# VectorE writes the result buffers once more ahead of the branch, and takes the minimum of the sums' test alone

## The chip, the cores and the metric

The kernel runs on one core of one Trainium2 chip. The core has five engines with a queue of instructions each: TensorE (PE in the profile: matrix products), VectorE (DVE), ScalarE (ACT), GpSimd (POOL) and SyncE (SP, which here issues nearly all transfers). They run on their own and wait for each other by semaphores. Transfers between the core's memory SBUF and the chip's memory are carried by 16 DMA engines; a transfer raises its semaphore by 16, one update from each. The metric is the device time of one execution in microseconds (us), as the median of several.

## The reference

One transformer block on 2048 rows of 448 numbers in bf16: a sliding-window attention and a gated feed-forward layer side by side, on the same normalised input.

```python
x = A_x
xn = _layernorm(x, axis=-1)
return x + _A_ref(xn, A_wqkv, A_wo) + _B_ref(xn, B_w_gate, B_w_up, B_w_down)
```

`_A_ref` has 16 heads of 28 columns; a row sees itself and the 255 rows before it, and the softmax of the scaled scores weighs v. `_B_ref` is `(gelu(x @ w_gate) * (x @ w_up)) @ w_down` with 1792 hidden columns.

## The kernel before

The rows are worked through in four blocks (`qb`) of 512. For each block the kernel computes the scores and their exponentials, multiplies with v, and computes the feed-forward layer's hidden columns (`hT`). The down projection of a block, which also takes in the attention's output projection, runs one block later beside the next one's attention, and for the last block at the very end. The order of the work on each engine is written out by hand (the pools are opened under `manual_schedule`), with generators that give out the work of TensorE in pieces of some 370 ns.

The softmax skips the usual subtraction of the row's maximum. That is right only while the sums of the exponentials stay in a range, so the kernel keeps all of them (`l_all`, 128 x 256) and tests them at the end. If any lies outside, it recomputes everything by `general_path`, a long second program under `tc.If`, which overwrites the output. With these inputs it doesn't run. The instructions of that program lie between the branch and the end of the kernel, so every engine has to jump over them.

The end of the kernel before goes like this:

- VectorE makes the test's 0 or 1 for every sum, and the minimum of each of the 128 partitions (`okc`, lines 802 to 805), and turns it into bf16 (`okb`, 806).
- `gen_down` gives the last block's down projection (lines 358 to 382): for each of four tiles of 128 rows 4 matmuls with `wo` (line 370) and 14 with `wd` (375) into one PSUM bank `po`, then VectorE's addition of x into the result buffer `res` (380), then SyncE's store of it (381). There are two `res` buffers, used in turn. The last tile is done in two halves of 224 columns, so the pass has five additions and stores.
- After a third of that work (`share`, then line 810) TensorE sums the 128 minima by a matmul of 1 x 1, `nok`; VectorE turns it into an integer `flag` (812).
- After another third, every engine loads the flag into a register (814, TENSOR_LOAD in the trace). ScalarE and GpSimd, which have no more work, load it and branch at once.
- The rest of the pass runs (`drain`), and each engine takes its branch (line 820). Behind the branch, on the side that skips the general path, every engine raises its own semaphore by as much as the general path would have (EVENT_SEMAPHORE of line 820), and SyncE does so for the eight semaphores of the stores, for each when the transfers so far have landed. Then comes the end of the program (line 927): SyncE waits in eight instructions for all semaphores, two in each, the sixth of which asks for VectorE's; all engines meet twice in a barrier; GpSimd clears the semaphores.

A hint to load the code behind the branch ahead of time stands in line 743, for VectorE and for TensorE.

Of the kernel before, what the change touches and what calls it, by code (L numbers as in the profile page):

```python
# [9 lines left out]
ALU = mybir.AluOpType  # L10
AX = mybir.AxisListType
bf16 = mybir.dt.bfloat16
f32 = mybir.dt.float32
i32 = mybir.dt.int32

S, D, H, Dh, F = 2048, 448, 16, 28, 1792
P = 128
NT = S // P
NF = F // P
QB, NB = 512, 4  # L20
# [34 lines left out]
def share(feeds, first, second):  # L55

    want = [first, second]
    while True:
        can = [i for i, f in enumerate(feeds) if f.gens and want[i] > 190 and not f.held]
        if not can:  # L60
            return
        i = max(can, key=lambda i: (not feeds[i].closed, want[i]))
        for f in feeds:
            if f is not feeds[i]:
                f.closed = False
        want[i] -= feeds[i].run()


def drain(feeds):

    while any(f.gens for f in feeds):
        min((f for f in feeds if f.gens), key=lambda f: (f.held, f.closed)).run()
# [3 lines left out]
def kernel(  # L76
# [11 lines left out]
    nc = tc.nc  # L88
    const = ctx.enter_context(tc.tile_pool(name="const", bufs=1))
# [3 lines left out]
    work = fast.enter_context(tc.tile_pool(name="work", bufs=3))  # L93
# [3 lines left out]
    phase = [None]  # L97
# [253 lines left out]
    DOWN = 4 * 3400  # L351
# [6 lines left out]
    def gen_down(qb, tags):  # L358

        hT, oN = hTs[qb], oNs[qb]  # L360
        for tt in range(4):
            t = 4 * qb + tt
            cs = slice(tt * P, (tt + 1) * P)
            for n, (lo, up) in enumerate(((0, D),) if t < NT - 1 else ((0, D // 2), (D // 2, D))):
                w = up - lo
                tag = tags[tt + n]
                down_tag[0] = tag
                po = psum.tile([P, QB], f32, name="po", tag=tag, bufs=2 if tag == "m" else 1)
                for g in range(4):
                    nc.tensor.matmul(po[:, 0:w], lhsT=oN[:, g, cs], rhs=wo[:, g, lo:up], start=(g == 0), stop=False,  # L370
                                     skip_group_check=True)
                    if g % 2:
                        yield 380 * w // D
                for f in range(NF):
                    nc.tensor.matmul(po[:, 0:w], lhsT=hT[:, f, cs], rhs=wd[:, f, lo:up], start=False, stop=(f == NF - 1),  # L375
                                     skip_group_check=True)
                    if f % 2 and f < NF - 1:
                        yield 375 * w // D
                res = work.tile([P, D], bf16, name="res", bufs=2)
                nc.vector.tensor_tensor(out=res[:, 0:w], in0=po[:, 0:w], in1=x_sb[:, t, lo:up], op=ALU.add)  # L380
                nc.sync.dma_start(out=outv[:, t, lo:up], in_=res[:, 0:w])
                yield 375 * w // D
# [412 lines left out]

    g1 = work.tile([P, 512], f32, name="g1", tag="wc", bufs=1)
    g2 = work.tile([P, 512], f32, name="g2", tag="wb", bufs=1)
    okc = const.tile([P, 1], f32, name="okc")
    okb = const.tile([P, 1], bf16, name="okb")
    one = const.tile([P, 1], bf16, name="one")  # L800
    lf = l_all[:, :, :].rearrange("p a b -> p (a b)")
    nc.vector.memset(one[:, :], 1.0)
    nc.vector.tensor_scalar(out=g1[:, 0:256], in0=lf, scalar1=L_LO, scalar2=None, op0=ALU.is_ge)
    nc.vector.scalar_tensor_tensor(out=g2[:, 0:256], in0=lf, scalar=L_HI, in1=g1[:, 0:256], op0=ALU.is_le, op1=ALU.mult)
    nc.vector.tensor_reduce(out=okc[:, :], in_=g2[:, 0:256], axis=AX.X, op=ALU.min)
    nc.vector.tensor_copy(out=okb[:, :], in_=okc[:, :])
    feed = Feed((gen_down(NB - 1, "dmomd" if last_tag[0] == "o" else "omdmo"), DOWN))
    share([feed], DOWN / 3, 0)
    nok = phase[0].pool.tile([P, 2 * QB], f32, name="nok", tag="s")
    nc.tensor.matmul(nok[0:1, 0:1], lhsT=okb[:, :], rhs=one[:, :], start=True, stop=True)  # L810
    flag = const.tile([1, 1], i32, name="flag")
    nc.vector.tensor_copy(out=flag[:, :], in_=nok[0:1, 0:1])
    share([feed], DOWN / 3, 0)
    n_ok = nc.values_load(flag[0:1, 0:1], min_val=0, max_val=P)
    drain([feed])
    phase[0].close()
    fast.close()


    with tc.If(n_ok < P, preferred_fallthrough_block=True, label="general"):  # L820
        general_path(tc, locals_=dict(x_sb=x_sb, xnT=xnT, qT=qT, kT=kT, v_sb=v_sb, wg=wg, wu=wu, wgu3=wgu3, wd=wd, wo=wo,
                                      ident=ident, outv=outv))

# [108 lines left out]
```

## Time and profile before

| What | us |
|---|---|
| median of 3 runs (lowest, highest) | 223.24 (223.16, 223.36) |
| the profiled execution, its own time | 223.5 |
| its span, first to last instruction | 221.7 |
| TensorE busy in the span | 214.3 |
| VectorE busy | 156.2 |
| VectorE's last addition (392 ns) starts | 217.37 |
| the last store is issued | 217.79 |

The profile is of one execution. Its page has the busy time of each engine, the chain of work that ended last, and the costliest groups of instructions; the trace behind it has every instruction, every DMA packet and every update of a semaphore. Times in it count from the first instruction of the span. Register loads, branches and semaphore instructions don't count as busy; they stand in the trace by their line, with an engine's name that ends in q. The packets of queue 1 are the kernel's own transfers, those of kind "instruction" (queues 8 and 14) are the engines' code. The granted clock of TensorE is 1.000 over the span.

### The profile page before, as it was taken

Reading aid. Unit: us, or ns where it says so; the run is one execution under the profiler, and the core shown is the slowest. Engines: PE = TensorE matmul, PEld = TensorE weight load, DVE = VectorE, ACT = ScalarE, POOL = GpSimd, SP = SyncE. Lnnn points to the kernel's source line nnn. Section 1 sums busy time; section 2 is a strip of 40 time slices with the busy share of each in tenths; the row PEclk is TensorE's granted clock in tenths of the full one; section 3 lists DMA queues with packets and bytes.
Section 4 is the critical chain, followed back from the end, with each engine's and each line's share of the span. In section 5 each row is a group of like instructions: output and inputs, shape, how many; then the busy total and the mean of one; then the engine's idle time right before and its main releaser. Section 6 shows DMA issues by size and latency. Waiting matters only on the chain.

```text
span 221.7 us, 5352 instructions
## 1 busy us (share of the span) xinstructions
PE 214.3 (97%) x2240; PEld 94.9 (43%) x2240; DVE 156.2 (70%) x370; ACT 132.9 (60%) x129; POOL 45.0 (20%) x65
## 2 busy tenths in 40 slices
PE   6999999999999999999999999999999999999992
PEld 2433333344444444444444445444344435444571
DVE  5889996799666983679566896495444899479320
ACT  4497788644878875432878886233567778464000
POOL 5773687320000220022000031022000022022000
PEclk9999999999999999999999999999999999999999
DMA  6997699104200001102500000200000000000011
GB/s 193 304 296 94 174 326 305 22 1 74 44 3 21 24 24 29 18 3 44 70 1 23 24 1 26 57 5 0 0 4 21 24 3 24 21 0 4 22 43 25
DMA packets 18044, 13.28 MB, mean 60 GB/s; under 512 B 8704, under 2 KB 16992, under 8 KB 18016
## 3 DMA queue, kind: packets, MB, share of 16 engines
q1 hardware_dynamic: 17072, 12.62, 22.6%
q8 instruction: 18, 0.29, 0.6%
q10 hardware_dynamic: 944, 0.29, 0.5%
q14 instruction: 10, 0.08, 0.1%
HBM read 9.15 MB, written 2.18 MB: 51 GB/s over the span
## 4 chain that ended last, share of the span: by engine, by line
PE 95%; DVE 2%; ACT 1%; POOL 0%; issue 0%; DVEq 0%
PE po L375 20%; PE gt L228 17%; PE u L228 12%; PE sc L600 6%; PE po L370 6%; PE gt L233 5%; PE ue L228 5%; PE ov L560 5%; PE pq L228 4%; PE pv L228 4%; PE pk L228 3%; PE wps L190 2%; PE pq L233 2%; PE ue L233 1%; PE pv L233 1%; PE s L228 1%
## 5 line engine op out<-in xcount | busy, mean ns | idle before, releaser
L604 ACT ACTIVATE p_sb<-sc 128x2048 bf16<-128x2048 f32 (+2 forms) x42 | 73.8, 1758 | 12.6 <-PE sc L600 7.3
L375 PE MATMUL po<-wd,hT 128*128 128x448 bf16 (+1 forms) x238 | 50.0, 342 | 0.0
L452 ACT ACTIVATE ge<-gt 128x1024 bf16<-128x1024 f32 x28 | 28.7, 1025 | 33.6 <-PE u L233 20.9
L527 POOL TENSOR_TENSOR oN<-oc,l 128x512 bf16<-128x512 f32 x12 | 16.0, 1332 | 138.6 <-DVE l L544 88.2
L228 PE MATMUL gt<-xnT,wg 128*128 128x512 bf16 x168 | 40.3, 380 | 0.0
L456 DVE TENSOR_TENSOR hT<-ge,u 128x512 bf16<-128x512 bf16 x40 | 25.6, 682 | 9.7 <-ACT ge L452 9.6
L375 PEld LDWEIGHTS <-hT 128*128 128x128 bf16 x238 | 21.4, 98 | 18.6 <-issue 2.6
L228 PE MATMUL u<-xnT,wu 128*128 128x512 bf16 x120 | 29.2, 379 | 0.0
L508 DVE TENSOR_TENSOR p_sb<-p_sb,masks 128x256 bf16<-128x256 bf16 (+1 forms) x90 | 27.2, 357 | 0.4 <-ACT p_sb L604 0.4
L228 PEld LDWEIGHTS <-wg 128*128 128x128 bf16 x168 | 15.1, 98 | 21.4 <-issue 5.2
L228 PEld LDWEIGHTS <-wu 128*128 128x128 bf16 x168 | 16.0, 98 | 19.2 <-issue 1.0
L549 DVE TENSOR_TENSOR oc<-oc,ov 128x512 f32<-128x512 f32 x12 | 8.3, 688 | 18.3 <-ACT oc L548 18.3
L600 PE MATMUL sc<-qT,kT 28*64 28x320 bf16 (+7 forms) x640 | 16.9, 263 | 0.1
L380 DVE TENSOR_TENSOR res<-po,x_sb 128x448 bf16<-128x448 f32 (+1 forms) x17 | 10.0, 586 | 8.7 <-PE po L375 8.6
L370 PE MATMUL po<-wo,oN 128*128 128x448 bf16 (+1 forms) x68 | 15.9, 342 | 0.0
L518 POOL TENSOR_SCALAR_AFFINE_SELECT p_sb<-p_sb 128x512 bf16<-128x512 bf16 (+1 forms) x20 | 14.3, 736 | 7.8 <-ACT p_sb L604 7.6
L409 DVE CAST hT<-ue 128x512 bf16<-128x512 f32 x16 | 10.2, 680 | 6.3 <-PE ue L233 6.2
L548 ACT COPY oc<-ov 128x512 f32<-128x512 f32 x12 | 7.0, 584 | 11.9 <-PE ov L560 11.9
L233 PE MATMUL gt<-xnT,wgu 64*128 64x512 bf16 x48 | 13.2, 379 | 0.0
L228 PE MATMUL pq<-xnT,wqp 128*128 128x512 bf16 x45 | 12.2, 380 | 0.3 <-DVE v_sb L253 0.3
L534 DVE STREAM_TRANSPOSE l<-oc 128x512 f32<-128x512 f32 x16 | 11.3, 704 | 1.4 <-POOL oN L527 1.2
L228 PE MATMUL ue<-xnT,wu 128*128 128x512 bf16 x48 | 12.0, 380 | 0.0
(87 smaller groups left out, 236.0 us busy)
## 6 DMA issues: line engine op xcount, KB each, us to landing
out_dram<-res SPq DMA_DIRECT2D x15, 112.0 KB
x_sb<-in_A_x_dram SPq DMA_DIRECT2D x3, 448.0 KB
wu<-in_B_w_up_dram SPq DMA_DIRECT2D x1, 1344.0 KB
wg<-in_B_w_gate_dram SPq DMA_DIRECT2D x1, 1344.0 KB
wd<-in_B_w_down_dram SPq DMA_DIRECT2D x3, 448.0 KB
wraw<-in_A_wqkv_dram SPq DMA_DIRECT2D x2, 252.0 KB
wo<-in_A_wo_dram SPq DMA_DIRECT2D x4, 98.0 KB
wv<-in_A_wqkv_dram SPq DMA_DIRECT2D x1, 336.0 KB
```

Of the source, the lines that this page charges most:

```text
L228: nc.tensor.matmul(ps, lhsT=lhs(c), rhs=rhs(c), start=start and c == 0, stop=stop and c == 2, skip_group_check=True)
L233: nc.tensor.matmul(ps, lhsT=lhs[p0:p0 + 64], rhs=rhs[p0:p0 + 64], start=start, stop=stop, tile_position=(p0, 0), skip_group_check=True)
L370: nc.tensor.matmul(po[:, 0:w], lhsT=oN[:, g, cs], rhs=wo[:, g, lo:up], start=(g == 0), stop=False, skip_group_check=True)
L375: nc.tensor.matmul(po[:, 0:w], lhsT=hT[:, f, cs], rhs=wd[:, f, lo:up], start=False, stop=(f == NF - 1), skip_group_check=True)
L452: nc.scalar.activation(out=ge[:, :, :], in_=pr["gt"][:, :, :], func=ACT.Gelu_apprx_tanh)
L456: nc.vector.tensor_tensor(out=hT[:, f + i, :], in0=ge[:, i, :], in1=u[:, :], op=ALU.mult)
L508: nc.vector.tensor_tensor(out=reg, in0=reg, in1=m, op=ALU.mult)
L518: nc.gpsimd.affine_select(out=reg, in_=reg, pattern=mid + [[1 if diag else -1, min(w, P)]], compare_op=ALU.is_ge, fill=0.0, base=0 if diag ...
L527: nc.gpsimd.tensor_tensor(out=oN[:, g, :], in0=oc[:, :], in1=inv, op=ALU.mult)
L534: nc.vector.transpose(out=l1[:, :, :].rearrange("p a b -> p (a b)"), in_=oc[:, :])
L600: nc.tensor.matmul(ss[k0:k0 + nk, j, col:col + nq], lhsT=kT[r, g, kt * P + k0:kt * P + k0 + nk], rhs=qT[r, g, qb * QB + q0:qb * QB + q0 + ...
L604: nc.scalar.activation(out=p_sb[:, :, 0:ncol], in_=ss[:, :, 0:ncol], func=ACT.Exp, scale=SCALE)
```

## The change

The minima of the 128 partitions are brought together by VectorE alone: the minima are put into the first column of a 128 x 32 field of ones, that is transposed in blocks of 32 x 32, a minimum along the rows gives one number for each block of 32 partitions, four copies bring these to one partition, and a last minimum and a conversion give the flag. The matmul `nok` is left out, and the two calls of `share` become one. The flag is now 0 or 1, and the branch compares it with 1. The small tiles `okc`, `okb` and `one` go; their successors are parts of the tile `g1`.

At the end, after `drain`, VectorE writes a zero into the first column of each of the two `res` buffers. A buffer may only be written when the store from it has landed, so the second of these waits for the last store; both stand ahead of VectorE's branch.

```diff
-    okc = const.tile([P, 1], f32, name="okc")
-    okb = const.tile([P, 1], bf16, name="okb")
-    one = const.tile([P, 1], bf16, name="one")
+    okc, okt, okm, okr, ok1 = g1[:, 256:288], g1[:, 288:320], g1[:, 320:321], g1[0:1, 324:328], g1[0:1, 328:329]
+    flag = const.tile([1, 1], i32, name="flag")
     lf = l_all[:, :, :].rearrange("p a b -> p (a b)")
-    nc.vector.memset(one[:, :], 1.0)
+    nc.vector.memset(okc, 1.0)
...
-    nc.vector.tensor_reduce(out=okc[:, :], in_=g2[:, 0:256], axis=AX.X, op=ALU.min)
-    nc.vector.tensor_copy(out=okb[:, :], in_=okc[:, :])
+    nc.vector.tensor_reduce(out=okc[:, 0:1], in_=g2[:, 0:256], axis=AX.X, op=ALU.min)
+    nc.vector.transpose(out=okt, in_=okc)
+    nc.vector.tensor_reduce(out=okm, in_=okt, axis=AX.X, op=ALU.min)
+    for i in range(4):
+        nc.vector.tensor_copy(out=okr[0:1, i:i + 1], in_=okm[32 * i:32 * i + 1, :])
+    nc.vector.tensor_reduce(out=ok1, in_=okr, axis=AX.X, op=ALU.min)
+    nc.vector.tensor_copy(out=flag[:, :], in_=ok1)
     feed = Feed((gen_down(NB - 1, "dmomd" if last_tag[0] == "o" else "omdmo"), DOWN))
-    share([feed], DOWN / 3, 0)
-    nok = phase[0].pool.tile([P, 2 * QB], f32, name="nok", tag="s")
-    nc.tensor.matmul(nok[0:1, 0:1], lhsT=okb[:, :], rhs=one[:, :], start=True, stop=True)
-    flag = const.tile([1, 1], i32, name="flag")
-    nc.vector.tensor_copy(out=flag[:, :], in_=nok[0:1, 0:1])
-    share([feed], DOWN / 3, 0)
-    n_ok = nc.values_load(flag[0:1, 0:1], min_val=0, max_val=P)
+    share([feed], DOWN * 2 / 3, 0)
+    n_ok = nc.values_load(flag[0:1, 0:1], min_val=0, max_val=1)
     drain([feed])
+    for _ in range(2):
+        nc.vector.memset(work.tile([P, D], bf16, name="res", bufs=2)[:, 0:1], 0.0)
     phase[0].close()
     fast.close()
...
-    with tc.If(n_ok < P, preferred_fallthrough_block=True, label="general"):
+    with tc.If(n_ok < 1, preferred_fallthrough_block=True, label="general"):
```

## The prediction

> **What bounds the kernel now.** I read the page first, then the chain that ended last, then the instructions of the branch (line 820) and of the end of the program (line 927), then what SyncE's queue waited for, and last the DMA packets of the final microseconds.
>
> ```profile
> span 221.7 us, 5352 instructions
> PE 214.3 (97%) x2240; PEld 94.9 (43%) x2240; DVE 156.2 (70%) x370; ACT 132.9 (60%) x129; POOL 45.0 (20%) x65
> ```
>
> TensorE is busy 97% of the span, so an instruction taken from its stream near the end shortens the span by its own length. The chain of the last pass:
>
> ```profile
> 206.87 0.76 PE po L370 x4
> 207.62 0.38 PE po L375 x2
> 208.00 0.09 PE nok L810
> 208.10 2.38 PE po L375 x12
> ...
> 211.23 2.65 PE po L375 x14
> ...
> 217.37 0.39 DVE res L380
> ```
>
> The matmul of the test, nok, stands in the middle of a row of po matmuls that runs without a gap to the last addition. After the addition 4 us of the span are left, in which no compute engine works. They belong to the last store, the branch and the closing barrier:
>
> ```profile
> L820 SPq EVENT_SEMAPHORE  x8: 17/17/17, 218.4 to 220.3; - x8
> L820 ACTq COMPARE_BRANCH  x1: 50/50/50, 208.8 to 208.8; - x1
> ...
> L820 ACTq EVENT_SEMAPHORE  x1: 17/17/17, 211.3 to 211.3; - x1
> ...
> L820 DVEq COMPARE_BRANCH  x1: 84/84/84, 217.4 to 217.4; - x1
> L820 DVEq EVENT_SEMAPHORE  x1: 21/21/21, 218.0 to 218.0; - x1
> ```
>
> ```profile
> L927 SPq EVENT_SEMAPHORE  x10: 17/28/28, 220.4 to 221.6; - x10
> ```
>
> ```profile
> SPq L820 <- SPq L820: 1.6, 2, 1.4
> ```
>
> Behind the branch SyncE has eight semaphore instructions of line 820, one for each store semaphore. Seven are done by 218.84; the eighth waits 1.4 us, until the last store has landed at 220.27. Then come eight waits of line 927, some 0.063 us apart, the barrier, and the end at 221.67. So the landing sets the end, and the end follows it by 1.40.
>
> Why does the store take 2.48 us from its issue at 217.79? One DMA packet of instructions begins at 218.58 and takes 0.70 (first line below, from 218.50 to 218.66). The second view is the DMA engines in three stretches behind it (its last two columns are DMA share and GB/s):
>
> ```profile
> q14 instruction: 1, 0.01, 27.4%
> ```
>
> ```profile
> 218.66:218.95 0.29, 0.00 (x0) 0.00 (x0) 0.00 (x0) 0.00 (x0) 0.00 (x0) 1.00 0.61 167
> 218.95:219.27 0.32, 0.00 (x0) 0.00 (x0) 0.00 (x0) 0.00 (x0) 0.00 (x0) 1.00 0.00 0
> 219.27:219.60 0.33, 0.00 (x0) 0.00 (x0) 0.00 (x0) 0.00 (x0) 0.00 (x0) 1.00 0.07 11
> ```
>
> The store's packets run until 218.95, then none, then nine more, the first at 219.276, as the instruction packet ends at 219.280: one of the 16 DMA engines had fetched code and kept its share of the store back. The semaphore's 16 updates say the same: 15 are there by 219.33 (1.54 after the issue), the sixteenth at 220.27. The other 16 stores to out bear it out. Nine have no instruction fetch among their packets, and their sixteenth update comes within 0.04 of the fifteenth (1.66 to 1.73 after the issue, at 112 KB). The seven whose packets met a fetch had one update late, by 0.36 to 2.1.
>
> Whose fetch is it? VectorE reaches its place behind the branch at 217.985 and the fetch begins 0.59 later. ScalarE reached its own at 211.300 and a fetch began at 211.901, 0.60 later. TensorE branches at 215.46 to 215.86 and a fetch of its queue begins at 216.63. SyncE's branch (218.17) is nearer in time, at 0.41, but SyncE jumps over few instructions and is at work again after 0.15. I take the fetch to be VectorE's, reading on behind the place it jumped to.
>
> **The change part by part.**
>
> *The matmul nok goes.* The po matmuls of 448 columns start every 0.189; those around nok start at 207.651, 208.030 and 208.230, that is 0.579 for what takes 0.379 without it. On the path: −0.20. All that follows it, the last addition and the last store, comes 0.20 earlier. The two calls that place the register loads spend the same 24 pieces of the last pass as the one call after, so these loads stay where they are.
>
> *More VectorE work for the test.* Two conversions (0.156 for okb, 0.146 for the flag) and a memset of 0.06 make way for a memset of 32 columns (0.085, from w3p's 128x32), a stream transpose of 128x32, three small minima, four copies of one element and a conversion. In the trace every small VectorE operation lies between 0.06 and 0.25; I take 0.15 each and 0.035 between dependent ones. From the end of the first minimum at 205.92 that is about 0.1 + 0.2 + 0.2 + 4 × 0.155 + 0.2 + 0.2, so the flag is there near 207.4. That is earlier than 208.28 now. The addition of the first tile of the pass, at 206.91 now, starts about half a microsecond later. Nothing needs it soon: its PSUM bank is wanted again for the last half tile (matmul at 215.44), its result buffer at 213.9. Cost on the path: 0. The first engine on the path that needs the flag is TensorE, which loads its register at 209.20 and would stand if it came later, so 1.8 us are to spare. Were each new operation as long as the 512-column transpose, 0.704, the flag would come near 211, 2 us too late; the rows of small operations are much nearer. ScalarE and GpSimd get the flag earlier and branch about 0.9 earlier. ScalarE's fetch at 209.77 then moves to about 208.9, onto the store of the first tile, which may land 1 us later; its buffer is needed 4 us after that. Cost: 0.
>
> *The two memsets.* The pool's next two result buffers are those of the two halves of the last tile, so the first memset waits for the next-to-last store and the second for the last. Behind them VectorE has only the branch, its semaphore instruction of line 820 and the barrier, so its branch moves from 217.38 to after the landing. Two things follow.
>
> First, the instruction fetch, which comes 0.59 after VectorE's arrival, can't meet the last store. That store then lands as its own 15 updates did, 1.54 plus up to 0.04: I take 1.57 in place of 2.48, −0.91. Bounds: −0.94, and 0 if the fetch isn't VectorE's. Other fetches there: TensorE's, which ends at 217.58, a microsecond before the store's packets.
>
> Second, VectorE comes late to the end. Call the landing L. A semaphore's update has released VectorE after 0.03 (216.233 to 216.261). If the wait stands in an instruction of its own, 0.10 more pass to the next (217.985 to 218.095), so the memset issues at L + 0.03 to 0.13; the branch 0.014 later, as behind the last addition, and it takes 0.084; from its end to VectorE's semaphore instruction 0.52 (217.465 to 217.985; the addition had ended at 217.76, so this was the branch and not a wait); 0.03 until others see it. SyncE's sixth wait of line 927 asks for that semaphore. It is at L + 0.40 now and would be held to L + 0.70 to 0.80. I take +0.35. From below the cost is 0: GpSimd and SyncE are back 0.13 and 0.15 after their branches, and with that VectorE is in time. From above: ScalarE needed 2.41 (208.893 to 211.300), which gives +2.25. I take VectorE's own 0.52, since it is the same branch to the same place with the same prefetch hint (line 743 is not touched, and the hint runs at 0.8 us).
>
> Sum: −0.20 − 0.91 + 0.35 = −0.76. The profiled execution took 223.5 (span 221.67 and 1.83 around it), so it would come to 222.74; the median of the runs is 0.26 below it, 223.24, which gives **222.48**.
>
> **The rivals.**
>
> *Slower: VectorE finds no code behind its branch.* ScalarE, which has no hint, shows the price: a fetch at 209.77 and 2.41 us from branch to next instruction. If VectorE's prefetched code is no longer there, because the test's added instructions shift the branch or because it sits 3 us longer, SyncE is held to L + 2.65: −1.11 + 2.25 = +1.14, 224.4. It decides once VectorE needs more than about 1.3 from branch to semaphore. For it: ScalarE's row. Against it: VectorE's 0.52, with no instruction packet between 211.90 and 216.63, so its code was there beforehand. The Trainium skill, "Runtime: NRT & Kernel Launch", section "Instruction fetch mechanics", has a taken branch out of the loaded pages stall until its target is fetched; ScalarE agrees with its 2.41, VectorE's 0.52 does not. Chance 0.10.
>
> *No change: the fetch stays.* If the packet at 218.58 is SyncE's, or another one falls on the store, only nok and the late arrival count: −0.20 + 0.35 = +0.15, 223.4. For it: the 0.41 from SyncE's branch. Against: the 0.59 and 0.60 above. Chance 0.16.
>
> *VectorE is in time.* −1.11, 222.1, if its way past the branch shrinks to SyncE's 0.15. Chance 0.06.
>
> *The fetch is missed at the end.* VectorE's fetch now begins near L + 1.3; by ScalarE's rows code is usable about 1.5 after a fetch begins (209.77 to 211.30), at L + 2.8, while the span ends at L + 1.75. If VectorE needs that block in the 1.83 around the span, up to 1 us comes back: 222.5 to 223.6. Nothing in the trace says where its block ends. Chance 0.08.
>
> **How the numbers follow.** The forecast has 0.60. Its own range, from the bounds of its terms (−0.84 to −0.65) and the 0.1 by which single runs stray, is 222.3 to 222.7. The range over the cases takes in "in time" below and "the fetch stays" above, 222.05 to 223.45, and leaves out the slower rival and the tails. A difference under 0.2% (0.45 us) is about what can't be told from no change here. Faster: 0.58 of the forecast, "in time", a little of the last rival: 0.65. Same: "the fetch stays" and parts of the last: 0.20. Slower: 0.15.
>
> **What would show it.** No nok, and po matmuls 0.189 apart through 208. VectorE's branch of line 820 behind the landing. No instruction packet between 218.3 and 219.1, one after 220. The last store's sixteenth update within 0.05 of the fifteenth, 1.57 after its issue. SyncE's waits of line 927 with one pause of about 0.35 at the sixth. I am wrong if the instruction packet still lies in the store, or if VectorE's semaphore instruction comes over 1.3 us behind its branch.

## The result, and the profile after

| What | before | after |
|---|---|---|
| median of 6 runs each, us (lowest, highest) | 223.32 (223.16, 223.52) | 222.53 (222.29, 223.04) |
| ratio, 95% interval | | 0.9965 [0.9953, 0.9977] |
| profiled execution, its own time | 223.5 | 223.04 |
| its span | 221.67 | 221.21 |
| last addition starts | 217.37 | 217.44 |
| from there to the end of the span | 4.30 | 3.78 |

The change takes 0.79 us off the time, where the forecast had 0.76 (222.48). Measured a second time it took off 0.54 (222.68 against 223.22, ratio 0.9972 [0.9961, 0.9982]). The sum came out right, but one step of it did not, as the experiments show.

The profiled execution is the longest of its six (the other spans are 220.5 to 220.8), so it has to be read with care. Its last pass is 0.27 later than that of before for a reason that lies ahead of the change: VectorE's statistics of the fifth tile are put together 10.31 us after the start before and at 10.57 here, and everything behind them keeps that distance. That hides the 0.20 of nok in this profile. The matmul itself is gone, as the timeline shows; the four copies of the test take the place of the conversion, and the first addition of the pass follows the flag at once:

```profile
206.69 0.61 DVE L808 COPY g<-g 1x1 f32<-1x1 f32 x4
...
206.98 0.92 PE L370 MATMUL po<-wo,oN 128*128 128x448 bf16 x4
207.34 0.14 DVE L809 TENSOR_REDUCE g<-g 1x1 f32<-1x4 f32 x1
207.51 0.14 DVE L810 CAST flag<-g 1x1 int32<-1x1 f32 x1
...
207.59 0.62 DVE L380 TENSOR_TENSOR res<-po,x_sb 128x448 bf16<-128x448 f32 x1
```

The branch (now line 821) and the writes (816):

```profile
L821 SPq EVENT_SEMAPHORE  x8: 17/17/17, 218.4 to 219.6; - x8
...
L821 DVEq COMPARE_BRANCH  x1: 84/84/84, 219.6 to 219.6; - x1
L821 DVEq EVENT_SEMAPHORE  x1: 21/21/21, 220.2 to 220.2; - x1
```

```profile
L816 DVE MEMSET res<- x2: 59/59/59, 219.5 to 219.6; 128x1 bf16 x2
L816 DVEq EVENT_SEMAPHORE  x1: 21/21/21, 219.4 to 219.4; - x1
```

VectorE's branch has moved from 217.4 to 219.6. From its end to VectorE's semaphore instruction it took 0.52 again (219.667 to 220.188). The instruction packet that lay in the last store at 218.58 now begins at 220.78, 0.60 behind that instruction (first line below, from 219.6 to 221.0). No instruction packet lies among the last store's packets (the same three stretches as before; the last columns are DMA share and GB/s):

```profile
q14 instruction: 1, 0.01, 2.3%
```

```profile
218.66:218.95 0.29, 0.00 (x0) 0.00 (x0) 0.00 (x0) 0.00 (x0) 0.00 (x0) 1.00 0.71 187
218.95:219.27 0.32, 0.00 (x0) 0.00 (x0) 0.00 (x0) 0.00 (x0) 0.00 (x0) 1.00 0.04 10
219.27:219.60 0.33, 0.00 (x0) 0.00 (x0) 0.06 (x1) 0.00 (x0) 0.00 (x0) 1.00 0.00 0
```

Nine late packets lay in the last of these stretches before; now there is none. The store's sixteenth update comes 1.69 after its issue in place of 2.48. SyncE then pauses once at the end, as the waits of its queue and the longest of its instructions of line 928 show:

```profile
SPq L821 <- SPq L821: 0.9, 3, 0.5
...
SPq L928 <- DVEq L821: 0.3, 1, 0.3
```

```profile
L928 SPq EVENT_SEMAPHORE  x10: 17/28/303, 219.6 to 221.1; - x10
```

So the end of the span follows the landing by 1.67 in place of 1.40. By these rows the forecast seems right in every term. One row speaks against it: line 816 has two writes but a single semaphore instruction, and that one waits for the next-to-last store's semaphore. The second write waits for no store. That VectorE branches behind the last landing here (219.58, the landing is at 219.54) is therefore not the work of the second write.

### The profile page after: what moved, and what is told of

Read it like the earlier page. It is cut to its first block, busy times and chain, and to the rows that moved or that the text cites. A ratio compares the mean times of both kernels' runs of the same rounds, so it can differ in the third digit from the quotient of the medians.

```text
span 221.2 us, 5334 instructions
## 1 busy us (share of the span) xinstructions
PE 212.0 (96%) x2214; PEld 95.1 (43%) x2239; DVE 157.6 (71%) x378; ACT 133.0 (60%) x129; POOL 45.0 (20%) x65
## 5 line engine op out<-in xcount | busy, mean ns | idle before, releaser
L228 PE MATMUL gt<-xnT,wg 128*128 128x512 bf16 x161 | 38.9, 380 | 1.0 <-issue 0.9
L228 PE MATMUL pq<-xnT,wqp 128*128 128x512 bf16 x36 | 11.7, 380 | 0.7 <-DVE v_sb L253 0.3
```

Of the source, the lines that this page charges most:

```text
L228: nc.tensor.matmul(ps, lhsT=lhs(c), rhs=rhs(c), start=start and c == 0, stop=stop and c == 2, skip_group_check=True)
```

## The experiments

Two questions were open: what each part of the change is worth, and whether VectorE's instruction fetch is what held the last store, or only the place of the wait. All ratios are to the kernel before on the same chip, in five rounds; a ratio isn't the quotient of the two medians beside it and can differ from it by up to 0.001.

**e1: the test without the writes.**

```diff
-    for _ in range(2):
-        nc.vector.memset(work.tile([P, D], bf16, name="res", bufs=2)[:, 0:1], 0.0)
```

> The changed kernel without the two writes into the result buffers: only the matmul nok is gone and VectorE makes the minimum alone. Theory of the forecast: only the 0.20 of nok are left of the gain, 223.1 us against 223.3 before; VectorE's instruction packet lies in the last store again and the store's sixteenth update comes 0.5 to 1 us after the fifteenth. Rival, the gain lies in the test and not in the writes: 222.5, as with the whole change.

Measured: 222.95 against 223.10, ratio 0.9994 [0.9985, 1.0003]. The last addition starts at 217.175, 0.19 earlier than in the kernel before. (That alone proves little: in the profiles without nok this point lies anywhere between 217.07 and 217.46.) VectorE branches at 217.2 again, and its instruction packet, of 0.46 this time, begins at 218.38, among the last store's packets:

```profile
q14 instruction: 1, 0.01, 2.9%
```

That row (of 218.2 to 219.2) has no counterpart in the same stretch after. The store's sixteenth update comes 2.13 after the issue, where it was 2.48 behind a packet of 0.70. The fetches are not of one length, and so neither is what they cost. (In this execution SyncE's issue of the store took 0.68 and not 0.33 as well, and the fifteenth update is late, 1.89. So the sixteenth is only 0.24 behind it, less than the 0.5 to 1 expected.) The gain does not lie in the test.

**e2: the writes without the test.**

```diff
     drain([feed])
+    for _ in range(2):
+        nc.vector.memset(work.tile([P, D], bf16, name="res", bufs=2)[:, 0:1], 0.0)
```

> The kernel before with the two writes alone; nok stays. Theory of the forecast: -0.91 for the landing and +0.30 to 0.35 for VectorE's late arrival, about -0.6, 222.7 us; no instruction packet of queue 14 between the issue of the last store and its landing. Rival, the writes only add a wait: 223.6 us, 0.3 slower than before.

Measured: 222.45 against 223.10, ratio 0.9971 [0.9961, 0.9982]: −0.65. This profile compares best with that of before, since its last addition starts at the same time, 217.367. The last store is issued at 217.786 and its sixteenth update comes 1.53 after that, 0.03 behind the fifteenth, so the landing gains 0.95. But SyncE does not pause at all, and the end follows the landing by 1.40, as before. The rows of its branch (line 822 here) say why:

```profile
L822 SPq EVENT_SEMAPHORE  x8: 17/17/17, 218.4 to 219.3; - x8
...
L822 DVEq COMPARE_BRANCH  x1: 84/84/84, 218.9 to 218.9; - x1
L822 DVEq EVENT_SEMAPHORE  x1: 21/21/21, 219.5 to 219.5; - x1
```

SyncE sees the last store land at 219.33, and VectorE has branched at 218.86, half a microsecond before. Both writes are done by 218.94, after the next-to-last store has landed (218.63) and before the last one has. So neither write waits for the last store, and there are two buffers: the second `work.tile` must have got the same one as the first. (e7 shows that a write into the buffer of the last store does wait.) Why the pool gave it out again isn't shown.

**e3: one write.**

```diff
-    for _ in range(2):
+    for _ in range(1):
```

> The changed kernel with the first of the two writes alone, which waits for the next-to-last store and not for the last. Theory: the next-to-last store lands 0.6 to 1.5 us after the last one is issued, so VectorE branches up to 0.9 earlier than with both writes, its fetch still starts behind the last store's packets, and SyncE waits for VectorE 0 to 0.2 in place of 0.30: 222.2 to 222.5 us. Rival, the 0.30 of SyncE's sixth wait is made up elsewhere and the end is set by the landing alone: no difference to the whole change, 222.5.

Measured: 222.34 against 223.10, ratio 0.9964 [0.9950, 0.9977], the whole change's 0.9965 and 0.9972. The store lands 1.55 after its issue and there is no pause. No cost and no gain of the second write shows.

**e7: a second write that waits for the last store.** This is the kernel that the forecast had in mind. `last_res[0]`, here and below, is the buffer of the pass's last store, kept by `gen_down`.

```diff
-    for _ in range(2):
-        nc.vector.memset(work.tile([P, D], bf16, name="res", bufs=2)[:, 0:1], 0.0)
+    nc.vector.memset(work.tile([P, D], bf16, name="res", bufs=2)[:, 0:1], 0.0)
+    nc.vector.memset(last_res[0][:, 0:1], 0.0)
```

> The changed kernel with its second write put into the buffer of the last store, by its name. (In the changed kernel the trace shows both writes waiting for the next-to-last store alone.) Now VectorE waits for the last store too, as the forecast had taken it. Theory: its branch comes after the landing L, its semaphore instruction at L + 0.70, SyncE's sixth wait of line 927 pauses for 0.30 where the changed kernel has no pause in most executions: about 0.3 slower than the whole change, 0.5 under the kernel before (ratio 0.998). Rival, the late arrival is hidden behind the barrier: as the whole change (0.9965).

Measured: 222.80 against 223.17, ratio 0.9985 [0.9973, 0.9996]: 0.13 to 0.2% more than the changed kernel. Each write now has a wait of its own, and the pause is there, at its full size (end 1.74 behind the landing, +0.35):

```profile
L817 DVEq EVENT_SEMAPHORE  x1: 21/21/21, 219.2 to 219.2; - x1
```

```profile
L818 DVEq EVENT_SEMAPHORE  x1: 21/21/21, 219.4 to 219.4; - x1
```

```profile
SPq L930 <- DVEq L823: 0.4, 1, 0.4
```

The profile alone doesn't part the two kernels, since its next-to-last store is late too (3.21 after its issue), and with that the changed kernel pauses as well, by 0.28. The times do, on the same chip and in the same rounds: e7's eleven executions took 222.58 or more, nine of the ten of the kernel with one copy below, which waits for no store, 222.52 or less (medians 222.80 and 222.44). A wait for the last store costs about what the forecast said, but the change does not have that wait.

**e4: no wait for a store.** VectorE's branch is put behind the end of the last addition by three copies, each of which reads the one before (and in a second kernel by one).

```diff
-    for _ in range(2):
-        nc.vector.memset(work.tile([P, D], bf16, name="res", bufs=2)[:, 0:1], 0.0)
+    src = last_res[0][:, 0:1]
+    for i in range(3):
+        nc.vector.tensor_copy(out=g2[:, 256 + i:257 + i], in_=src)
+        src = g2[:, 256 + i:257 + i]
```

> The changed kernel with three one-column copies on VectorE in place of the two writes, the first of which reads the last addition's result and each of the others the one before. VectorE's branch then comes about 0.4 us after the addition has ended, waits for no store, and its fetch starts some 1.6 us after the last store's issue, 0.4 behind its packets; its semaphore instruction comes 1.0 us after the issue, in time for SyncE. Theory: -0.20 -0.91, 222.2 us. Rival, only a branch behind the landing keeps the store free: 223.1 us, as without the writes.

> As e4 with one copy in place of three: VectorE branches when the last addition has ended, 0.4 us later than in the kernel before and 0.4 earlier than in e4. Its fetch begins 1.22 us after the last store's issue, the store's packets end at 1.16. Theory: even this is enough, as e4 (ratio 0.996), with a fetch that touches the packets in a few executions. Rival, the free store needs a wait for a store: 222.95, as without the writes (0.9994).

Measured: with three copies 222.26 against 223.10, ratio 0.9959 [0.9945, 0.9972]; with one 222.44 against 223.17, ratio 0.9967 [0.9956, 0.9978]. The fetch begins 1.62 and 1.49 after the last store's issue, behind its packets, and the store lands 1.65 and 1.54 after it. With one copy VectorE's branch and its semaphore instruction are these:

```profile
L825 DVEq COMPARE_BRANCH  x1: 84/84/84, 217.8 to 217.8; - x1
...
L825 DVEq EVENT_SEMAPHORE  x1: 21/21/21, 218.4 to 218.4; - x1
```

The 1.49 had been expected at 1.22, which would have been 0.06 behind the store's packets; in this profile the fetch came 0.86 after VectorE's semaphore instruction and not 0.59, and why is open. One of the ten executions took 223.37, more than the median of the kernel before, and has no profile; the expectation had foreseen a few in which the fetch still touches the packets. So no wait for a store is needed: a branch 0.4 later than before, at the end of the last addition in place of its start, is enough, in nine executions of ten by their times. That the time follows the place of VectorE's branch with three different means (writes, one copy, three copies), and is lost without any of them (e1), shows that the fetch is VectorE's and that it is what held the store.

**e5: no prefetch hint for VectorE.** The writes stay, so its branch still comes late; only the hint is gone.

```diff
-        if qb in (1, 3):
+        if qb in (3,):
```

> The changed kernel without the prefetch hint for VectorE (the one for TensorE stays). Theory: VectorE, like ScalarE, then fetches the code behind its branch when it gets there and needs 2.4 us in place of 0.52; it branches about 1.1 us after the last store's issue, so its semaphore instruction comes near 3.6 where SyncE asks for it at 1.95: 1.6 us slower than the whole change, 0.85 slower than the kernel before (ratio 1.004). Its fetch begins 0.9 after the branch, near the landing. Rival, the 0.52 doesn't come from the hint: as the whole change (0.9965).

Measured: 224.53 against 223.17, ratio 1.0051 [1.0038, 1.0064], where 1.004 had been expected. A packet of instructions begins 0.96 after the branch, and VectorE goes on 2.80 after it (218.880 to 221.680), where ScalarE's 2.41 had been expected. SyncE stands at its sixth wait:

```profile
SPq L928 <- DVEq L821: 2.2, 1, 2.2
```

This is the slower rival, made to happen: the late branch costs so little only because of the hint. The Trainium skill, "Runtime: NRT & Kernel Launch", section "Instruction fetch mechanics", says that a taken branch out of the loaded pages stalls until its target is fetched. The runs agree for VectorE and ScalarE without a hint (2.80 and 2.41). With a hint VectorE has no such stall (0.52), and GpSimd and SyncE, which have no hint either, are back 0.13 and 0.15 after their branches in the kernel before. No row tells which of the targets were loaded by then.

**e6: TensorE's branch late as well.** To e4's three copies a product of one column is added, which makes TensorE's branch wait for the last addition.

```diff
+    late = phase[0].pool.tile([P, 2 * QB], f32, name="late", tag="s")
+    nc.tensor.matmul(late[0:1, 0:1], lhsT=last_res[0][:, 0:1], rhs=last_res[0][:, 0:1], start=True, stop=True)
```

> The three copies of e4 (no wait for a store) and on TensorE a product of one column of the last addition's result, ahead of its branch, so that TensorE's branch too comes after the last addition and its 16 KB instruction packet (0.95 us) behind the packets of the last two stores. Theory: the next-to-last store's sixteenth update comes within 0.05 of its fifteenth, and so does the last one's in every execution; the median 0 to 0.1 under e4 (ratio 0.995 to 0.996), with less spread. Rival, TensorE's late branch holds SyncE's seventh wait as VectorE's held the sixth: 0.3 or more slower than e4.

Measured: 222.44 against 223.17, ratio 0.9962 [0.9949, 0.9975]; no gain over e4, and no less spread either (0.30 from lowest to highest, 0.29 there). TensorE branches at 217.6 in place of 215.3. Its packet of 16 KB, which begins between 216.3 and 217.4 in the other profiles, now begins at 218.82, behind the stores' last packet (218.74):

```profile
q1 hardware_dynamic: 144, 0.06, 22.1%
q8 instruction: 1, 0.02, 5.9%
```

(the packets between 218.0 and 219.0). For the first time the next-to-last store is free too: its sixteenth update comes 1.54 after its issue, where it comes at 2.56 to 3.27 in the other profiles. But in this kernel VectorE doesn't wait for that store, and SyncE waits for the last one anyway. TensorE's late branch costs nothing either.

**The changed kernel and three copies side by side.** The two were run once more on one chip.

> The changed kernel as it is, once more, beside a2. In its first profile TensorE's instruction packet began at 217.35, 1.2 us after the next-to-last store's issue, and both last stores were late; in the profile with the writes alone it began 0.57 after it and only the next-to-last store was. Theory: the usual execution is of the second kind; the last store's sixteenth update then comes within 0.05 of the fifteenth, VectorE's semaphore instruction comes before SyncE asks for it, the span is 220.5 to 220.6 and the time 222.3 to 222.5. Rival: the first profile is the usual one, and SyncE pauses 0.3 at the sixth wait: span near 221.

> The three copies of e4 once more, on the same chip as the changed kernel. Theory: equal to it in usual executions, and up to 0.3 faster in those in which the next-to-last store is late, since VectorE waits for no store: the median 0 to 0.1 lower. Rival: e4's lead of 0.1 was the chip's or the hour's, no difference.

Measured: the changed kernel 222.68 against 223.22, ratio 0.9972 [0.9961, 0.9982]; three copies 222.59, ratio 0.9968 [0.9956, 0.9980]. The difference of 0.1 is inside both intervals, so three copies are not shown to be better. The profile of the changed kernel is again like its first one (packet of TensorE 1.45 long, next-to-last store 3.15 after its issue, pause of 0.30, span 221.17), against my expectation of the usual one. Its execution is the second longest of eight; one other span is 221.2 too, the remaining six are 220.7 to 220.9. Both profiles of the changed kernel thus show the pause. How often it comes in the executions whose spans alone are known is not settled; by their lengths it is the rarer case. In the three copies' profile TensorE's packet is as late, the last store lands 1.74 after its issue, and there is no pause: end 1.40 behind the landing.

## Why the prediction was right, and where it was not

*The matmul nok: −0.20.* Right by the trace: the po matmuls start 0.189 apart through the place. The times fit but are too coarse to show it: e1 is lower by 0.13 (0.06% ± 0.09%).

*More VectorE work: 0 on the path.* Right. From the end of the first minimum to the flag 1.47 us passed, where about 1.5 had been worked out. The transpose took 0.21 and the second minimum 0.19; the copies came 0.155 apart. (The list of new operations in the prediction has three small minima; there are two, and its sum has two.) ScalarE's fetch moved onto the first tile's store as foreseen (sixteenth update 0.77 behind the fifteenth), and nothing waited for it.

*The fetch no longer meets the last store: −0.91.* Right as a mechanism, which was shown by e1, e2 and e4. Its size is that of the one execution it was read from: −0.95 between the profiles of before and e2. By the medians the writes are worth 0.65 (e2), and 0.5 to 0.65 as the difference of the whole change (0.9965, 0.9972) and e1 (0.9994). Three copies, which wait for no store and so have no late arrival in them, are 0.69 below e1 on the same chip and in the same rounds (222.26, 222.95). The fetch in the profile of before was the longest of VectorE's last fetches in the twelve profiles, 0.70 (the others took 0.31 to 0.55; that of e1 0.46). The prediction had a hint of this: the profiled execution lay 0.26 above the median, and the forecast took the whole 0.91 over to the median all the same. A cost read off one collision is one draw.

*"So the first memset waits for the next-to-last store and the second for the last."* This is the step that failed, and the description of the change ahead of the prediction has it wrong in the same way. The second write went to the buffer of the first, so both come after the next-to-last store alone (e2, and line 816 of after). From it followed *"Second, VectorE comes late to the end"*, +0.35 in every execution. In the profiles this pause comes only where the next-to-last store is held back, behind an instruction packet of TensorE, until the last has nearly landed. That is so in the two profiles of the changed kernel (landing 3.15 and 3.22 after the issue, +0.28 at the end), and not in those of e2 and e3 (2.57, no pause). The price itself was about right: e7, which does wait for the last store, shows +0.35 in its profile and takes 0.3 to 0.45 us more than the changed kernel by the two ratios (their intervals overlap), and 0.36 more than one copy in the same rounds.

The two errors have opposite signs and nearly cancel: the gain of the landing was taken 0.2 to 0.3 too large, and the late arrival, which is there in some executions, was charged to all. That the sum of −0.76 came so near to −0.79 is luck; the second measurement has −0.54. (The prediction's own range goes by −0.84 to −0.65; the bounds of its terms give −0.84 to −0.70, which moves its upper end by 0.05.)

*The rivals.* "VectorE finds no code" did not come: 0.52 before and after. e5 shows that it was a real one, at 2.80. "The fetch stays" fell with the packet at 220.78. "VectorE is in time" was given 0.06 for a shorter branch; it holds in e2 and e3 for another reason, the missing wait. "The fetch is missed at the end" did not show: the time around the span is 1.83 after as before.

*The rest of the list.* Of the forecast's signs, the sixteenth update "within 0.05 of the fifteenth" held in e2 and e3, not in the profile of after, where it was 0.14 behind. There TensorE's packet had held the next-to-last store until 219.35. That the part of the last store on the same DMA engine had to queue behind that is likely, but the trace doesn't name the engines.

## What to carry to other kernels

In these runs an engine that jumps fetches more code some 0.6 us after it has arrived, and that packet runs on one of the DMA engines that carry the kernel's stores: where the end of a kernel hangs on a store, look for instruction packets between its issue and its landing, and move the branch of the engine that causes them by a few dependent instructions. A wait meant for one buffer of a pool should be looked up in the instructions: a second tile asked for at once can be the same buffer. And a collision seen in one profile is one draw of its size; take its value over several executions.

## What the runs showed of the hardware

- A store's semaphore gets 15 of its 16 updates within 0.13 to 0.19 us. The sixteenth tells whether an instruction packet lay among the store's packets: 0.01 to 0.04 later without one (9 stores of the profile before), 0.36 to 2.1 later with one (8 stores). The Trainium skill, "DMA: Bandwidth & Descriptors", section "Queues, rings and completion order", says that a DMA engine takes whole packets from its queues in turn; the rows agree, with instruction packets of 0.31 to 1.7 us.
- From an engine's first instruction at its new place to its next instruction packet it is 0.59 to 0.63 (VectorE in eleven of twelve profiles, ScalarE in ten). The three others have 0.86 (VectorE, one copy), 0.87 and 0.90 (ScalarE, e4 with three copies and e6).
- With a hint, branch to next instruction is 0.52 on VectorE in all profiles that have it, wherever the branch stands; without one it is 2.80 (VectorE, e5) and 2.41 to 2.88 (ScalarE), but 0.13 on GpSimd.
- TensorE's fetch at the end is not fixed: with its branch at 215.2 to 215.6, its packet began between 216.3 and 217.4 and took 0.95 to 1.46.
